# Attention, an FFT block and a gated MLP on one core: rows in six chunks of 384 instead of eight of 320 and 256, with another order of the last products and of the first loads

## The chip, the cores and the metric

The kernel runs on one NeuronCore of a Trainium2 chip. Its engines are TensorE (PE; its weight loads are shown as PEld), VectorE (DVE), ScalarE (ACT), GpSimd (POOL) and SyncE (SP), which here only issues DMAs. The metric is the device time of one execution in microseconds. Before the change the median of three runs is 808.04 us (806.26 to 809.92).

## The reference, cut to what matters

Inputs: q, k, v of (4, 8, 576, 64), weights of three parts, all float32; 4 batches of 576 rows are 2304 rows of 512 columns.

```python
scores = q @ k.T / 8;  keep 0 <= i - j < 64;  attn = softmax(scores)
x = (attn @ v) as (4, 576, 512)
u = x + real(fft(fft(x, axis=1), axis=2))
un = (u - mean(u)) / sqrt(var(u) + 1e-6)
x = u + relu(un @ w_ch1) @ w_ch2                    # 512 -> 2048 -> 512
h = gelu_tanh(x @ w_in);  g, v = h[..., :512], h[..., 512:]
v_s = w_sg @ layernorm(v) * g_ln + b_sg             # over the 576 rows of a batch
out = x + (g * v_s) @ w_out
```

## The kernel before, in words

Every product that needs full precision is made of three (`mm3`, lines 118 to 120): operands are kept as a rounded part and a remainder (`xh`, `xl` for the rows, `hi`, `lo` in the weight sets), and high x high, high x low and low x high are added up in PSUM. Rows lie transposed in SBUF: `uT` is one tile of 128 partitions x 4 x 2304 rows and holds the running sum all the way.

The rows are cut into chunks (`CHUNKS`): per batch one of 320 and one of 256, eight in all. A chunk is the moving operand of one product, so its size is the number of columns that a product streams. Each chunk has its own pair of tiles `xh[n]`, `xl[n]`.

- *Attention* (from line 248) takes blocks of 64 queries, 36 in all, in a pipeline of scores, transposes, products with v, normalization and a transpose back into `uT`. `load_q`, `load_k` and `load_v` issue all their loads from SP's queue; the mask is loaded between two pieces of the first k. Beside attention two lanes run: `weights()` decodes the first three weight sets and `work()` runs the Fourier step `dft(0)`, the layer norm `ln(0)`, `dft(1)` and `ln(1)`.
- *Layer norm* (`ln(n)`) takes a chunk in pieces of up to 128 rows: transposes of `uT` (L509), a copy, the statistics on DVE, one power on POOL, the scaling on ACT, transposes back (L528), two copies on ACT into `xh` (L531, L532) and a subtraction on POOL into `xl` (L533).
- *MLP* (`mlp`) goes by phases (`PHASES`): hidden blocks 0 to 3, then 4 and 5, over the first half of the chunks, the same over the second half, then 6 to 9, 10 to 12 and 13 to 15 over all. For each chunk and hidden block f there are 12 products into `h`, relu on ACT (L581), the remainder on DVE (L582), and, two steps later, 12 products into `acc`; at the end of a phase four adds on DVE bring `acc` into `uT` (L562). Ahead of each chunk `before(g, n)` sees to it that the chunk's layer norm has been written into the program. The lane `rest()` holds what is still missing at the start: the decode of set 3, `ln(2)` and `ln(3)` woven with `dft(2)`, `dft(3)`, and then the norms of the second half.
- *gMLP*: `gate_u` over all chunks, then per batch `v_tiles` (products of 512 columns), `spatial` (the product over a batch's 576 rows, in halves of 320 and 256, whose result goes back into `xh`, `xl`) and `project`, two chunks per batch, whose residual comes from memory (`x2`) through `ctemp` and whose result is stored from SP's queue.

The order on each engine is made by a planner when the program is built: instructions stand in the order in which the Python code emits them, moved forward by priorities (`high_priority`, `SOON`, `URGENT`), and each engine then runs its list strictly in order. `drive` only decides in which order lanes emit.

Of the kernel before, what the change touches and what calls it, by code (L numbers as in the profile page):

```python
# [20 lines left out]
NF = FF // 128  # L21
TOK = B * S
CA, CB = 320, 256
CHUNKS = [(S * b + o, n) for b in range(B) for o, n in ((0, CA), (CA, CB))]
NCH = len(CHUNKS)
P0 = 4
HEAD, TAIL = range(NCH // 2), range(NCH // 2, NCH)
PHASES = [(range(P0), HEAD), (range(P0, 6), HEAD), (range(P0), TAIL), (range(P0, 6), TAIL),
          (range(6, 10), range(NCH)), (range(10, 13), range(NCH)), (range(13, 16), range(NCH))]
URGENT = 5000  # L30
# [71 lines left out]
class Kernel:  # L102
# [101 lines left out]
    def load_k(self, b, g):  # L204
        t = self.ap_.tile([128, 4, 256], F32, tag="k", bufs=3, name="k")
        o = 192 * g
        for c in (slice(0, 128), slice(128, 256)) if b == g == 0 else (slice(0, 256),):
            self.nc.sync.dma_start(t[:, :, c], self.aps["k"][b, :, :, o + c.start:o + c.stop])
            if b == g == c.start == 0:
                self.nc.sync.dma_start(self.mask, self.aps["mask"])  # L210
        self.kt[b, g] = t

    def load_q(self, b, j, w):

        t, o = self.qring[(b * 5 + j // 2) % QB], j % 2
        for h in range(2):
            dst = t[64 * h:64 * h + 64, o:o + w, :, h].rearrange("d n a q -> d (n a) q")
            self.nc.sync.dma_start(dst, self.aps["q"][b, h, :, j:j + w].rearrange("d n a q -> d (n a) q"))
        for i in range(w):
            self.qt[b, j + i] = t[:, o + i]  # L220

# [274 lines left out]
    def ln(self, n):  # L496
        nc, p = self.nc, self.lp
        V, A = nc.vector, nc.scalar
        start, size = CHUNKS[n]
# [24 lines left out]
        for i, (o, r) in enumerate(parts):  # L524
            ps = self.gtile()
            pv = ps[:].rearrange("p (k t) -> p k t", k=4)[:, :, 0:r]
            for k in range(4):
                nc.tensor.transpose(pv[:, k], us[i][:r, 128 * k:128 * k + 128], self.ident[:r, :r])  # L528
            hi = self.xh[n][:, :, o:o + r]
# [3 lines left out]
            nc.gpsimd.tensor_tensor(out=self.xl[n][:, :, o:o + r], in0=cp, in1=hi, op=ALU.subtract)  # L533
            yield 1000


# [5 lines left out]
    def mlp(self, before):  # L542
# [26 lines left out]
        for g, (fs, ns) in enumerate(PHASES):  # L569
            for n in ns:  # L570
                before(g, n)
                xh, xl, size = self.xh[n], self.xl[n], CHUNKS[n][1]
                for f in fs:
# [4 lines left out]
                    rh = self.bp.tile([128, CA], F32R, tag="rh", bufs=3, name="rh")[:, 0:size]  # L578
                    rl = self.bp.tile([128, CA], F32R, tag="rl", bufs=3, name="rl")[:, 0:size]
# [31 lines left out]
    def ctemp(self):  # L611
        self.ndec += 1
        if self.ndec % 3 == 0:
            return self.cp.tile([128, CA], F32, tag="res", name="res")
        s = self.pers.tile([128, 256, 2], I32, tag="dec_s", bufs=2, name="dec_s")
        return s[:].rearrange("p a b -> p (a b)").bitcast(F32)[:, 0:CA]

    def ctile(self):
        self.nct += 1
# [36 lines left out]
    def v_tiles(self, b):  # L656
# [3 lines left out]
        V, A = nc.vector, nc.scalar  # L660
        o = b % 2
        if o == 0:
            for d, x in ((self.xt_h, self.xh), (self.xt_l, self.xl)):
                for e in range(2):
                    nc.gpsimd.tensor_scalar(out=d[:, :, 64 * e:64 * e + 64], in0=x[2 * (b + e)][:, :, 256:320], scalar1=1.0, scalar2=None, op0=ALU.mult)
        for i in range(5 if o == 0 else 4):
            ps = self.ctile()
            terms = []
            for k in range(4):
                if i < 4:  # L670
                    n, t = 2 * b + i // 2, slice(128 * (i % 2), 128 * (i % 2) + 128)
                    lh, ll = self.xh[n][:, k, t], self.xl[n][:, k, t]
# [25 lines left out]
    def spatial(self, b):  # L698
# [2 lines left out]
        o = b % 2  # L701
        tail = self.vtail[o]
        for h in range(2):
            n = 2 * b + h
            start, size = CHUNKS[n]
            for c in range(4):
                s = slice(128 * c, 128 * c + 128)
                ps = self.ctile()[:, 0:size]
# [5 lines left out]
                t = self.pers.tile([128, CA], I32, tag="dec_w", bufs=2, name="dec_w")[:, 0:size].bitcast(F32)  # L714
                V.scalar_tensor_tensor(out=t, in0=ps, scalar=self.gT[:, c:c + 1], in1=self.bbc[:, CA * h:CA * h + size], op0=ALU.mult, op1=ALU.add)
                V.tensor_tensor(out=t, in0=t, in1=ug, op=ALU.mult)
                A.activation(out=self.xh[n][:, c], in_=t, func=AF.Copy)
                V.tensor_tensor(out=self.xl[n][:, c], in0=t, in1=self.xh[n][:, c], op=ALU.subtract)
                yield 6 * size

    def project(self, b):
        nc = self.nc
        for h in range(2):
            n = 2 * b + h
            start, size = CHUNKS[n]
            for c in range(4):
                s = slice(128 * c, 128 * c + 128)
                res = self.ctemp()[:, 0:size]
                nc.sync.dma_start(res, self.x2[:, c, start:start + size])
                ps = self.ctile()[:, 0:size]  # L730
                self.mm3(ps, [(self.w_out(k)[0][:, s], self.w_out(k)[1][:, s], self.xh[n][:, k], self.xl[n][:, k]) for k in range(4)])
                o = self.uT[:, c, start:start + size]
                nc.vector.tensor_tensor(out=o, in0=ps, in1=res, op=ALU.add)
                if n == NCH - 1:
                    nc.sync.dma_start(self.aps["out"][:, c, start:start + size], o)
                yield 5 * size
            if n < NCH - 1:
                nc.sync.dma_start(self.aps["out"][:, :, start:start + size], self.uT[:, :, start:start + size])
# [20 lines left out]
def emit(tc, aps):  # L759
    with ExitStack() as ctx:  # L760
# [19 lines left out]
        def work():  # L780
            for b in range(2):
                yield from when(scaled(k.dft(b)), lambda: k.xdone >= b)
                yield from scaled(k.ln(b))

        def weights():
            yield W0
# [1 line left out]
                yield from spaced(k.decode_f(f), W1)  # L788

        k.open_x(0, k.lp)  # L790
        k.open_x(1, k.lp)
        fill = [[weights()], [work()]]
        drive(k.attention(), *fill)
        for f in sum(fill, []):
# [2 lines left out]
        k.attn_es.close()  # L797
        p, es = k.pool("early", side="right")
        ctx.enter_context(es)
        for n in HEAD[2:]:  # L800
            k.open_x(n, p)
        for i in (3, 4, 5):
            k.open_set(i, p)
        k.open_mlp()
# [17 lines left out]
                    else:  # L822
                        yield w / 2

        def norm(*ns):
            for n in ns:
                yield from soon(k.ln(n))
                done.add(n)

        def rest():  # L830
            yield from soon(k.decode_f(3))
            done.update((0, 1))
            yield from weave(norm(2, 3), soon(k.dft(2)))
            yield from soon(k.dft(3))
            k.dft_es.close()
            p, es = k.pool("late", side="left")
            ctx.enter_context(es)
            for n in TAIL:
                k.open_x(n, p)
            for i in (6, 7):  # L840
                k.open_set(i, p)
            for n in TAIL:
# [70 lines left out]
def layout(q, k, v, w1, w2, w_in, g, w_sg, b_sg, w_out):  # L913
# [19 lines left out]
    o["sg"] = ca(np.concatenate([st[:256], st[320:], st[256:320], st[256:320]]).reshape(5, 128, S))  # L933
    o["g"] = ca(g.reshape(4, 128).T)
    o["b"] = ca(b_sg.reshape(1, S))
    o["tab"] = tables()
# [22 lines left out]
```

## Time and profile before

| | us |
|---|---|
| median of three runs | 808.04 |
| profiled execution, its time | 806.52 |
| profiled execution, its span | 804.8 |
| TensorE busy | 780.5 |
| VectorE busy | 463.2 |
| ScalarE busy | 322.0 |
| GpSimd busy | 203.0 |

The span is the time from the first to the last instruction of the profiled execution; busy times are sums over an engine's instructions. Matmuls are pipelined: a shown duration is longer than the distance to the next one, and the distance between starts is what a product costs. "Idle before, releaser" names what ended an engine's wait.

### The profile page before, as it was taken

Reading aid. Unit: us, or ns where it says so; the run is one execution under the profiler, and the core shown is the slowest. Engines: PE = TensorE matmul, PEld = TensorE weight load, DVE = VectorE, ACT = ScalarE, POOL = GpSimd, SP = SyncE. Lnnn points to the kernel's source line nnn. Section 1 sums busy time; section 2 is a strip of 40 time slices with the busy share of each in tenths; the row PEclk is TensorE's granted clock in tenths of the full one; section 3 lists DMA queues with packets and bytes.
Section 4 is the critical chain, followed back from the end, with each engine's and each line's share of the span. In section 5 each row is a group of like instructions: output and inputs, shape, how many; then the busy total and the mean of one; then the engine's idle time right before and its main releaser. Section 6 shows DMA issues by size and latency. Waiting matters only on the chain.

```text
span 804.8 us, 15475 instructions
## 1 busy us (share of the span) xinstructions
PE 780.5 (97%) x6084; PEld 751.3 (93%) x6084; DVE 463.2 (58%) x1110; ACT 322.0 (40%) x774; POOL 203.0 (25%) x258
## 2 busy tenths in 40 slices
PE   7989699999999999999999999999999999999998
PEld 6878588989999999999999999999999998989898
DVE  4888958795286347952226823643240358565653
ACT  4877687763345434421114411333232243131310
POOL 2144536574333223310003200232250020010000
PEclk9999899999999999999999999999999999999999
DMA  8996632230021003320002400132130020303042
GB/s 252 346 272 178 180 101 68 66 104 15 2 64 43 1 15 106 118 79 1 2 1 79 131 1 1 42 115 88 44 126 11 1 60 1 118 1 118 1 118 94
DMA packets 59320, 63.70 MB, mean 79 GB/s; under 512 B 22384, under 2 KB 42736, under 8 KB 59248
## 3 DMA queue, kind: packets, MB, share of 16 engines
q1 hardware_dynamic: 58672, 59.75, 24.9%
q0 software_dynamic: 576, 2.97, 1.1%
q8 instruction: 48, 0.79, 0.4%
q14 instruction: 24, 0.20, 0.1%
HBM read 53.25 MB, written 9.44 MB: 78 GB/s over the span
## 4 chain that ended last, share of the span: by engine, by line
PE 80%; DVE 10%; DMA 4%; ACT 3%; issue 2%; SPq 1%; POOL 1%; DVEq 0%; ACTq 0%
PE acc L118 7%; PE acc L119 7%; PE acc L120 7%; PE h L118 7%; PE h L120 7%; PE h L119 7%; PE c L118 6%; PE c L119 6%; PE c L120 6%; PE g L118 3%; PE g L119 3%; PE g L120 3%; PE sc L262 3%; DMA dec_s<-in_wo 2%; PE pv L290 2%; DVE dec_w L156 2%
## 5 line engine op out<-in xcount | busy, mean ns | idle before, releaser
L118 PE MATMUL h<-xh,set 128*128 128x256 f32 (+1 forms) x512 | 151.7, 297 | 0.7 <-DVE rl L582 0.5
L118 PE MATMUL acc<-rh,set 128*128 128x256 f32 (+1 forms) x512 | 151.5, 296 | 0.8 <-DVE uT L562 0.7
L120 PE MATMUL h<-xh,set 128*128 128x256 f32 (+1 forms) x512 | 151.5, 296 | 0.0
L119 PE MATMUL h<-xl,set 128*128 128x256 f32 (+1 forms) x512 | 151.0, 295 | 0.0
L120 PE MATMUL acc<-rh,set 128*128 128x256 f32 (+1 forms) x512 | 150.8, 294 | 0.0
L119 PE MATMUL acc<-rl,set 128*128 128x256 f32 (+1 forms) x512 | 150.7, 294 | 0.0
L160 POOL TENSOR_TENSOR set<-dec_w,set 128x256 fp32r<-128x256 f32 x88 | 69.6, 797 | 230.7 <-ACT set L159 230.4
L582 DVE SCALAR_TENSOR_TENSOR rl<-h,rh 128x320 fp32r<-128x320 f32 (+1 forms) x128 | 58.0, 453 | 119.3 <-ACT rh L581 118.8
L581 ACT ACTIVATE rh<-h 128x320 fp32r<-128x320 f32 (+1 forms) x128 | 51.7, 404 | 138.9 <-PE h L120 101.5
L118 PEld LDWEIGHTS acc<-rh,set 128*128 128x128 f32 x512 | 96.5, 188 | 1.8 <-issue 1.7
L118 PEld LDWEIGHTS h<-xh,set 128*128 128x128 f32 x512 | 96.5, 189 | 1.5 <-DVE rl L582 1.4
L120 PEld LDWEIGHTS h<-xh,set 128*128 128x128 f32 x512 | 96.7, 189 | 0.0
L119 PEld LDWEIGHTS h<-xl,set 128*128 128x128 f32 x512 | 96.6, 189 | 0.0
L119 PEld LDWEIGHTS acc<-rl,set 128*128 128x128 f32 x512 | 96.4, 188 | 0.1
L120 PEld LDWEIGHTS acc<-rh,set 128*128 128x128 f32 x512 | 96.4, 188 | 0.0
L562 DVE TENSOR_TENSOR uT<-acc,uT 128x320 f32<-128x320 f32 (+1 forms) x160 | 61.8, 449 | 16.5 <-PE acc L120 16.5
L154 ACT ACTIVATE dec_g<-dec_s 128x256 f32<-128x256 f32 x88 | 38.0, 438 | 63.4 <-DVE dec_w L156 28.1
L491 POOL TENSOR_TENSOR rq<-rq,mhalf 128x1 f32<-128x1 f32 (+2 forms) x26 | 17.0, 653 | 159.7 <-DVE rq L490 156.6
L155 DVE TENSOR_SCALAR dec_w<-dec_s 128x256 int32<-128x256 int32 x88 | 36.9, 424 | 34.5 <-POOL set L160 23.0
L120 PE MATMUL c<-xh,set 128*128 128x256 f32 (+1 forms) x188 | 55.4, 295 | 0.0
L119 PE MATMUL c<-xl,set 128*128 128x256 f32 (+1 forms) x188 | 55.4, 295 | 0.0
L118 PE MATMUL c<-xh,set 128*128 128x256 f32 (+1 forms) x188 | 55.4, 295 | 0.0
(195 smaller groups left out, 1661.9 us busy)
## 6 DMA issues: line engine op xcount, KB each, us to landing
dec_s<-in_w SPq DMA_DIRECT2D x64, 256.0 KB, 2.8
v<-in_v SPq DMA_DIRECT2D x16, 520.0 KB, 4.7
k<-in_k SPq DMA_DIRECT2D x11, 512.0 KB, 5.7
dec_s<-in_wi SPq DMA_DIRECT2D x16, 256.0 KB, 2.6
q<-in_q SPq DMA_DIRECT2D x30, 128.0 KB, 5.4
x<-uT SPq DMA_DIRECT2D x4, 640.0 KB, 3.9
out<-uT SPq DMA_DIRECT2D x4, 640.0 KB, 4.0
dec_s<-in_wo SPq DMA_DIRECT2D x8, 256.0 KB, 2.8
```

The source lines that it names most:

```text
L118: mm(out, lhsT=lh, rhs=rh, start=first and i == 0, stop=False)
L119: mm(out, lhsT=lh, rhs=rl, start=False, stop=False)
L120: mm(out, lhsT=ll, rhs=rh, start=False, stop=last and i == n - 1)
L154: nc.scalar.activation(out=g, in_=s[:, :, 1].bitcast(F32), func=AF.Copy, scale=2.0 ** -112)
L155: nc.vector.tensor_scalar(out=w, in0=s[:, :, 0], scalar1=29, scalar2=None, op0=ALU.logical_shift_right)
L156: nc.vector.scalar_tensor_tensor(out=w, in0=g[:].bitcast(I32), scalar=3, in1=w, op0=ALU.logical_shift_left, op1=ALU.bitwise_or)
L160: (eng or nc.gpsimd).tensor_tensor(out=lo[:, o:o + 256], in0=f, in1=hi[:, o:o + 256], op=ALU.subtract)
L262: nc.tensor.matmul(sc[:, hp], lhsT=q[:, hp].rearrange("p a b -> p (a b)"), rhs=k[:, hp, o:o + 128], start=True, stop=True)
L491: self.nc.gpsimd.tensor_tensor(out=y, in0=v, in1=self.mhalf[:m, 0:n], op=ALU.pow)
L562: V.tensor_tensor(out=x, in0=acc[:, c, 0:size], in1=x, op=ALU.add)
L581: A.activation(out=rh, in_=o, func=AF.Relu)
L582: V.scalar_tensor_tensor(out=rl, in0=o, scalar=0.0, in1=rh, op0=ALU.max, op1=ALU.subtract)
```

## The change: what it does

Chunks become six of 384 rows, which cross the borders of the batches: chunk 1 holds the end of batch 0 and the start of batch 1, chunk 4 the end of batch 2 and the start of batch 3. Chunk 0 keeps its own tiles; chunks 1 and 2 share one pair (`open_pair`), 3 to 5 another (`open_tail`); `pieces` and `piece` find the part of a tile for a stretch of rows. `work()` no longer runs a second layer norm beside attention: `ln(1)` and `ln(2)` both stand in `rest()`, woven with `dft(2)`. `v_tiles` takes a batch's rows in plain order (the table `sg` is laid out to match), `spatial` keeps its halves and splits a result where a tile ends. `project` goes by chunk: chunk 0 after batch 0, chunks 1 and 2 after batch 1, 3 after batch 2, 4 and 5 after batch 3. The mask, and the second half of q for the first four blocks, are issued from ACT's queue.

```diff
-CHUNKS = [(S * b + o, n) for b in range(B) for o, n in ((0, CA), (CA, CB))]
+CHUNKS = [(384 * i, 384) for i in range(6)]
+X0 = 1152
+UNITS = CHUNKS
-HEAD, TAIL = range(NCH // 2), range(NCH // 2, NCH)
+HEAD, TAIL = range(3), range(3, NCH)
...
-                self.nc.sync.dma_start(self.mask, self.aps["mask"])
+                self.nc.scalar.dma_start(self.mask, self.aps["mask"])
...
-            self.nc.sync.dma_start(dst, self.aps["q"][b, h, :, j:j + w].rearrange("d n a q -> d (n a) q"))
+            eng = self.nc.scalar if h and b == 0 and j < 4 else self.nc.sync
+            eng.dma_start(dst, self.aps["q"][b, h, :, j:j + w].rearrange("d n a q -> d (n a) q"))
...
+    def open_tail(self, p):
+        h, l = (p.tile([128, 4, TOK - X0], F32R, name=f"x{x}t") for x in "hl")
+        for n in TAIL:
+            o, size = CHUNKS[n][0] - X0, CHUNKS[n][1]
+            self.xh[n], self.xl[n] = h[:, :, o:o + size], l[:, :, o:o + size]
+    def pieces(self, t0, n):
+        for a, z, tiles in ((0, 384, 0), (384, X0, 1), (X0, TOK, 2)):
+            i, j = max(t0, a), min(t0 + n, z)
+            if i < j:
...
+                yield i - t0, j - i, h[:, :, i - a:j - a], l[:, :, i - a:j - a]
...
-                A.activation(out=self.xh[n][:, c], in_=t, func=AF.Copy)
-                V.tensor_tensor(out=self.xl[n][:, c], in0=t, in1=self.xh[n][:, c], op=ALU.subtract)
+                for i, r, xh, xl in self.pieces(start, size):
+                    A.activation(out=xh[:, c], in_=t[:, i:i + r], func=AF.Copy)
+                    V.tensor_tensor(out=xl[:, c], in0=t[:, i:i + r], in1=xh[:, c], op=ALU.subtract)
...
-                yield from scaled(k.ln(b))
+                if b == 0:
+                    yield from scaled(k.ln(b))
...
-            done.update((0, 1))
-            yield from weave(norm(2, 3), soon(k.dft(2)))
+            done.add(0)
+            yield from weave(norms(1, 2), soon(k.dft(2)))
...
-            drive(k.project(b), [])
+            for n in ((0,), (1, 2), (3,), (4, 5))[b]:
+                drive(k.project(n), [])
```

## Rows read from the trace of the kernel before

**Rows 1.** The page's first part: busy time of each engine.

```profile
PE 780.5 (97%) x6084; PEld 751.3 (93%) x6084; DVE 463.2 (58%) x1110; ACT 322.0 (40%) x774; POOL 203.0 (25%) x258
```

**Rows 2.** Windows: length, busy PE, PEld, DVE, ACT, POOL, granted clock, DMA share, GB/s.

```profile
0.00:20.00 20.00, 14.87 (x107) 13.78 (x108) 9.03 (x17) 8.64 (x22) 4.88 (x21) 0.91 0.85 252
...
80.00:100.00 20.00, 12.94 (x113) 10.48 (x110) 18.21 (x39) 13.02 (x33) 10.96 (x12) 0.83 0.63 183
...
145.00:180.00 35.00, 32.91 (x243) 30.98 (x242) 31.92 (x63) 24.53 (x63) 23.27 (x25) 1.00 0.30 89
180.00:300.00 120.00, 120.00 (x918) 118.44 (x917) 64.34 (x169) 52.70 (x116) 40.52 (x48) 1.00 0.08 24
...
760.00:804.80 44.80, 41.59 (x311) 41.09 (x309) 23.06 (x60) 5.98 (x12) 1.27 (x2) 0.99 0.31 95
```

**Rows 3.** The page's groups: MLP products of line 118, both chunk sizes together.

```profile
L118 PE MATMUL h<-xh,set 128*128 128x256 f32 (+1 forms) x512 | 151.7, 297 | 0.7 <-DVE rl L582 0.5
L118 PE MATMUL acc<-rh,set 128*128 128x256 f32 (+1 forms) x512 | 151.5, 296 | 0.8 <-DVE uT L562 0.7
```

**Rows 4.** Timeline (start, duration, instruction): last project, first of 320, first and last of 256.

```profile
788.74 0.31 PE L118 MATMUL c<-xh,set 128*128 128x320 f32 x1
...
795.78 0.28 PE L118 MATMUL c<-xh,set 128*128 128x256 f32 x1
...
801.31 0.28 PE L120 MATMUL c<-xh,set 128*128 128x256 f32 x1
```

**Rows 5.** Timeline: first of 48 products of 512 in v_tiles, and the project product behind them.

```profile
670.17 0.40 PE L118 MATMUL c<-set,xh 128*128 128x512 f32 x1
...
681.30 0.31 PE L118 MATMUL c<-xh,set 128*128 128x320 f32 x1
```

**Rows 6.** Timeline of PE at the end of attention: ln(1)'s transposes, a wait.

```profile
136.17 1.10 PE L509 MATMUL g<-ident,uT 128*128 128x128 f32 x8
137.10 0.60 PE L277 MATMUL pt<-ident,s 128*128 128x128 f32 x4
...
141.13 1.12 PE L290 MATMUL pv<-v,pts 128*64 128x65 f32 x16 [1.42 <-DVE rs L494]
```

**Rows 7.** Timeline of the start: ACT's table load, SP's issues, first exponentials, a wait.

```profile
0.72 1.28 ACT L270 ACT_TABLE_LOAD   x1 [0.72 <-PEq L946]
...
0.73 1.48 SPq L218 DMA_DIRECT2D q<-in_q  x2
...
7.52 0.57 SPq L208 DMA_DIRECT2D k<-in_k  x1
...
9.07 1.28 ACT L270 ACTIVATE s<-s,mx 128x128 f32<-128x128 f32 x4 [7.06 <-DVE mx L268]
...
13.37 1.13 PE L262 MATMUL sc<-k,q 128*128 128x128 f32 x8 [1.71 <-DMA k<-in_k]
```

**Rows 8.** Timeline: ln(2)'s first transposes, its last subtraction, its chunk's first product.

```profile
144.18 1.09 PE L509 MATMUL g<-ident,uT 128*128 128x128 f32 x8
...
174.98 0.74 POOL L533 TENSOR_TENSOR xl<-u,xh 128x256 fp32r<-128x256 f32 x1
...
179.91 0.31 PE L118 MATMUL h<-xh,set 128*128 128x320 f32 x1
```

**Rows 9.** Timeline behind v_tiles(1): a project add, the last vl, the first spatial product.

```profile
686.78 0.49 DVE L733 TENSOR_TENSOR uT<-c,dec_s 128x320 f32<-128x320 f32 x1
687.34 0.69 DVE L689 TENSOR_TENSOR vl<-u,set 128x512 fp32r<-128x512 f32 x1
...
693.99 0.31 PE L118 MATMUL c<-set,set 128*128 128x320 f32 x1
```

**Rows 10.** Timeline's last add; DMA issues: count, KB each, us to landing.

```profile
801.63 0.42 DVE L733 TENSOR_TENSOR uT<-c,dec_s 128x256 f32<-128x256 f32 x1 [0.49 <-PE c L120]
...
dec_s<-x SPq DMA_DIRECT2D x10, 160.0 KB, 2.3
...
out<-uT SPq DMA_DIRECT2D x4, 128.0 KB, 2.0
```

More of the change, by code (lines that the diff above doesn't have):

```diff
@@ L23 @@
 CA, CB = 320, 256
-CHUNKS = [(S * b + o, n) for b in range(B) for o, n in ((0, CA), (CA, CB))]
+CHUNKS = [(384 * i, 384) for i in range(6)]
 NCH = len(CHUNKS)
+X0 = 1152
+UNITS = CHUNKS
+UNITS_OF = [(n,) for n in range(NCH)]
 P0 = 4
-HEAD, TAIL = range(NCH // 2), range(NCH // 2, NCH)
+HEAD, TAIL = range(3), range(3, NCH)
 PHASES = [(range(P0), HEAD), (range(P0, 6), HEAD), (range(P0), TAIL), (range(P0, 6), TAIL),
@@ L476, in open_x, with open_pair, piece @@
         self.xl[n] = p.tile([128, 4, CHUNKS[n][1]], F32R, name=f"xl{n}")
+    def open_pair(self, p):
+        h, l = (p.tile([128, 4, X0 - 384], F32R, name=f"x{x}m") for x in "hl")
+        for n in (1, 2):
+            o, size = CHUNKS[n][0] - 384, CHUNKS[n][1]
+            self.xh[n], self.xl[n] = h[:, :, o:o + size], l[:, :, o:o + size]
+        self.xmid = h, l
+    def open_tail(self, p):
+        h, l = (p.tile([128, 4, TOK - X0], F32R, name=f"x{x}t") for x in "hl")
+        for n in TAIL:
+            o, size = CHUNKS[n][0] - X0, CHUNKS[n][1]
+            self.xh[n], self.xl[n] = h[:, :, o:o + size], l[:, :, o:o + size]
+        self.xtail = h, l
+    def pieces(self, t0, n):
+        for a, z, tiles in ((0, 384, 0), (384, X0, 1), (X0, TOK, 2)):
+            i, j = max(t0, a), min(t0 + n, z)
+            if i < j:
+                h, l = ((self.xh[0], self.xl[0]), getattr(self, "xmid", None), getattr(self, "xtail", None))[tiles]
+                yield i - t0, j - i, h[:, :, i - a:j - a], l[:, :, i - a:j - a]
+    def piece(self, t0, n):
+        (_, _, h, l), = self.pieces(t0, n)
+        return h, l
     def open_set(self, i, p):
@@ L498, in ln @@
         V, A = nc.vector, nc.scalar
-        start, size = CHUNKS[n]
+        start, size = UNITS[n]
         parts = [(o, min(128, size - o)) for o in range(0, size, 128)]
@@ L528, in ln @@
                 nc.tensor.transpose(pv[:, k], us[i][:r, 128 * k:128 * k + 128], self.ident[:r, :r])
-            hi = self.xh[n][:, :, o:o + r]
+            hi, lo = self.piece(start + o, r)
             cp = us[i][:, 0:4 * r].rearrange("p (k t) -> p k t", k=4)
@@ L532, in ln @@
             A.activation(out=hi, in_=cp, func=AF.Copy)
-            nc.gpsimd.tensor_tensor(out=self.xl[n][:, :, o:o + r], in0=cp, in1=hi, op=ALU.subtract)
+            nc.gpsimd.tensor_tensor(out=lo, in0=cp, in1=hi, op=ALU.subtract)
             yield 1000
@@ L577, in mlp @@
                     self.mm3(o, [(t[:, 0, 128 * k:128 * k + 128], t[:, 1, 128 * k:128 * k + 128], xh[:, k], xl[:, k]) for k in range(4)])
-                    rh = self.bp.tile([128, CA], F32R, tag="rh", bufs=3, name="rh")[:, 0:size]
-                    rl = self.bp.tile([128, CA], F32R, tag="rl", bufs=3, name="rl")[:, 0:size]
+                    rh = self.bp.tile([128, 384], F32R, tag="rh", bufs=3, name="rh")[:, 0:size]
+                    rl = self.bp.tile([128, 384], F32R, tag="rl", bufs=3, name="rl")[:, 0:size]
                     with self.tc.high_priority(URGENT):
@@ L613, in ctemp @@
         if self.ndec % 3 == 0:
-            return self.cp.tile([128, CA], F32, tag="res", name="res")
+            return self.cp.tile([128, 512], F32, tag="res", name="res")
         s = self.pers.tile([128, 256, 2], I32, tag="dec_s", bufs=2, name="dec_s")
-        return s[:].rearrange("p a b -> p (a b)").bitcast(F32)[:, 0:CA]
+        return s[:].rearrange("p a b -> p (a b)").bitcast(F32)
     def ctile(self):
@@ L662, in v_tiles @@
         if o == 0:
-            for d, x in ((self.xt_h, self.xh), (self.xt_l, self.xl)):
-                for e in range(2):
-                    nc.gpsimd.tensor_scalar(out=d[:, :, 64 * e:64 * e + 64], in0=x[2 * (b + e)][:, :, 256:320], scalar1=1.0, scalar2=None, op0=ALU.mult)
+            for e in range(2):
+                for d, x in zip((self.xt_h, self.xt_l), self.piece(S * (b + e) + 512, 64)):
+                    nc.gpsimd.tensor_scalar(out=d[:, :, 64 * e:64 * e + 64], in0=x, scalar1=1.0, scalar2=None, op0=ALU.mult)
         for i in range(5 if o == 0 else 4):
@@ L670, in v_tiles @@
                 if i < 4:
-                    n, t = 2 * b + i // 2, slice(128 * (i % 2), 128 * (i % 2) + 128)
-                    lh, ll = self.xh[n][:, k, t], self.xl[n][:, k, t]
+                    lh, ll = (x[:, k] for x in self.piece(S * b + 128 * i, 128))
                 else:
@@ L703, in spatial @@
         for h in range(2):
-            n = 2 * b + h
-            start, size = CHUNKS[n]
+            start, size = S * b + CA * h, (CA, CB)[h]
             for c in range(4):
@@ L716, in spatial, with project @@
                 V.tensor_tensor(out=t, in0=t, in1=ug, op=ALU.mult)
-                A.activation(out=self.xh[n][:, c], in_=t, func=AF.Copy)
-                V.tensor_tensor(out=self.xl[n][:, c], in0=t, in1=self.xh[n][:, c], op=ALU.subtract)
+                for i, r, xh, xl in self.pieces(start, size):
+                    A.activation(out=xh[:, c], in_=t[:, i:i + r], func=AF.Copy)
+                    V.tensor_tensor(out=xl[:, c], in0=t[:, i:i + r], in1=xh[:, c], op=ALU.subtract)
                 yield 6 * size
-    def project(self, b):
+    def project(self, n):
         nc = self.nc
[L723 to L738, printed above, removed]
+        start, size = CHUNKS[n]
+        for c in range(4):
+            s = slice(128 * c, 128 * c + 128)
+            res = self.ctemp()[:, 0:size]
+            nc.sync.dma_start(res, self.x2[:, c, start:start + size])
+            ps = self.ctile()[:, 0:size]
+            self.mm3(ps, [(self.w_out(k)[0][:, s], self.w_out(k)[1][:, s], self.xh[n][:, k], self.xl[n][:, k]) for k in range(4)])
+            o = self.uT[:, c, start:start + size]
+            nc.vector.tensor_tensor(out=o, in0=ps, in1=res, op=ALU.add)
+            if n == NCH - 1:
+                nc.sync.dma_start(self.aps["out"][:, c, start:start + size], o)
+            yield 5 * size
+        if n < NCH - 1:
+            nc.sync.dma_start(self.aps["out"][:, :, start:start + size], self.uT[:, :, start:start + size])
 def drive(main, *lanes):
@@ L790, in emit @@
         k.open_x(0, k.lp)
-        k.open_x(1, k.lp)
         fill = [[weights()], [work()]]
@@ L799, in emit @@
         ctx.enter_context(es)
-        for n in HEAD[2:]:
-            k.open_x(n, p)
+        k.open_pair(p)
         for i in (3, 4, 5):
@@ L823, in weave, with norms, norm @@
                         yield w / 2
-        def norm(*ns):
+        def norms(*ns):
             for n in ns:
-                yield from soon(k.ln(n))
-                done.add(n)
+                yield from norm(n)
+        def norm(n):
+            for u in UNITS_OF[n]:
+                yield from soon(k.ln(u))
+            done.add(n)
         def rest():
             yield from soon(k.decode_f(3))
-            done.update((0, 1))
-            yield from weave(norm(2, 3), soon(k.dft(2)))
+            done.add(0)
+            yield from weave(norms(1, 2), soon(k.dft(2)))
             yield from soon(k.dft(3))
@@ L837, in rest @@
             ctx.enter_context(es)
-            for n in TAIL:
-                k.open_x(n, p)
+            k.open_tail(p)
             for i in (6, 7):
@@ L932, in layout @@
     st = w_sg.T
-    o["sg"] = ca(np.concatenate([st[:256], st[320:], st[256:320], st[256:320]]).reshape(5, 128, S))
+    o["sg"] = ca(np.concatenate([st, st[512:]]).reshape(5, 128, S))
     o["g"] = ca(g.reshape(4, 128).T)
```

## The prediction

> **What bounds the kernel now.** I read the page's first part, then the windows by stage, and only then the timeline. The first part shows TensorE busy 97% of the span and no other engine above 58% [rows 1]. The windows show where most of the other 24 us lie: TensorE has gaps in the attention stage (5.1 us in the first 20, 7.1 us at 80 to 100, where VectorE is busy 18.2 of 20 us), 2.1 us at 145 to 180, none from 180 to 300, and 3.2 us in the last stretch, nearly all of it the drain of the last output [rows 2]. The reader is to see that from 145 us on the time is the count of products times their spacing, at a granted clock of 1.00 (2.4 GHz): only fewer or closer products help there, and every new wait costs its full length. In the 35 us where the MLP starts VectorE is busy 31.9 us, so that is where something can come late.
>
> **1. Six chunks instead of eight.** Line 118 issues every third product of the MLP: 512 h and 512 acc over eight chunks [rows 3], so 128 per chunk; gate_u and project add 4 x 4 each by their loops; 160 times three lines make 480 products per chunk. The columns stay 2304 in all, so what can be saved is the part of the spacing that does not go with columns. From the timeline: 48 products of 320 start between 788.74 and 795.78, 146.7 ns each; those of 256 behind them take 5.53 us over 47 steps, 117.7 ns [rows 4]; 48 of 512 take 11.13 us, 231.9 ns [rows 5]. No row has 384 columns.
> - Lower bound of the spacing: 320's own surplus over its columns at 2.4 GHz (146.7 - 133.3) kept, 160 + 13.4 = 173.4 ns.
> - Between 320 and 512: 146.7 + 64 x 85.2/192 = 175.1 ns.
> - On from 256 through 320: 146.7 + 29.0 = 175.7 ns.
>
> A weight tile costs 4 x (146.7 + 117.7) = 1057.6 ns now; six of 384 cost 1040, 1051 or 1054 ns. Times 480: -8.4, -3.4 or -1.6 us. 320 is the nearest row, but its surplus grows to 18.6 ns at 512, so I take 174.5 ns: 1047 ns, **-5.1 us**. Wider relu and add instructions lie in longer steps of 4.2 us (24 x 0.1745), with more room for both; nothing is counted for them.
>
> **2. Fewer and later layer norms.** Twenty pieces of rows become 18. The two that go are those of ln(1) ahead of the MLP: 8 transposes from 136.17 to the next product at 137.10 [rows 6], and 8 back, as long: **-1.9 us**. With their VectorE steps goes part of the 1.4 us for which the products of 141.13 waited behind rs (L494) [rows 6]: 0 to -1.4, I take **-0.5 us**. What is late next there is the last pv itself.
>
> **3. The start.** SP issues one DMA after another, 6.8 us of them before the k block that the products at 13.37 wait 1.7 us for [rows 7]. Moved off SP are the mask and three q halves. A q issue is 0.74 us of SP's time (two in 1.48), so everything behind the four is issued up to 3.0 us sooner. On ACT's queue they stand behind the table load (0.72 to 2.00) and end near 5.0 us; the first activation comes at 9.07, having waited for VectorE, so ACT pays nothing. Were that cover gone, 3 us of issues would lie before the first exponential. POOL's queue is not passed by anything. The transfers share one set of engines (share 0.85 of the first 20 us [rows 2]), so the k block will not land by the whole 3 us sooner: 0 to -1.7 us (its wait gone), I take **-1.0 us**.
>
> **4. The norm that is due sooner.** Before, chunks 0 and 1 were normalized when the MLP began, and ln(2) had from 144.18 (its first transposes) to 175.72 (its last subtraction on POOL), 31.5 us; its chunk's first product came at 179.91, behind two chunks [rows 8]. Now only chunk 0 is ready, and ln(1) has to take that way while chunk 0 runs. TensorE's work before chunk 1 must begin, worked out from spacings shown above: 72 products of chunk 0, 72 x 0.1745 = 12.6 us; the 24 that normally follow later, 4.2 us, if the planner draws them ahead; dft(2)'s first stage, 39 products of 256 or 258 columns at 118 ns, 4.6 us; the norm's 24 transposes at 0.116, 2.8 us; the next norm's first eight, 0.9 us; and the start of dft(2)'s second stage, 8 products of 290 columns at some 133 ns, 1.1 us. Together 26.2 us against 31.5: a hole of 5.3 us. Of those 35 us, 2.1 are idle already [rows 2] and would fall into the hole; and without chunk 1's relu steps the norm itself should be a little sooner. Bounds: 0 (norm ready in 26 us) and +11.5 us (no work drawn ahead: 12.6 + 4.6 + 2.8 = 20.0 against 31.5). I take **+2.0 us**. Chunk 2 then has a further 16.8 us and dft's rest for ln(2), whose transposes already begin under ln(1): nothing.
>
> **5. The gMLP's order.** Spatial steps and v_tiles keep their shapes. Project's products cover the end of v_tiles: its last vl ends at 688.03, 6.7 us after the first project product at 681.30, and spatial began at 693.99 [rows 5, 9]. project(0) and project(3) are now 48 products, 8.4 us, instead of 12.7: still 1.7 us more than needed; nothing, with +1 us as the upper end. The eight extra small copies and subtractions where a spatial half crosses row 384 lie beside some 1.6 us of products each. At the end both last chunks stand behind spatial(3): chunk 4 needs only its first half, and its 8.4 us cover the chain to chunk 5. The very end grows: the add takes 0.42 us for 256 columns and 0.49 for 320 [rows 9, 10], so about 0.55; a store of 128 KB lands in 2.0 us and a load of 160 KB in 2.3 [rows 10], so 192 KB in some 2.3 to 2.6: **+0.5 us**.
>
> **Sum.** -5.1 - 1.9 - 0.5 - 1.0 + 2.0 + 0.5 = -6.0 us. The profiled execution took 806.52 us (span 804.8), 1.5 under the median of three, 808.04. The same step from each: 800.5 and 802.0. I forecast **802.0 us**, with 798 to 805.5 as this case's own range. A measurement of this kernel can tell some 0.5%, 4 us: faster is below 804.0, slower above 812.1.
>
> **Rivals.**
> - *The spacing goes with the columns, and fewer chunks save next to nothing.* For it: the surplus over 2.4 GHz is 11.0, 13.4 and 18.6 ns at 256, 320 and 512 [rows 4, 5], so a straight line through the ends leaves only 3.5 ns per product, and the line through 256 and 320 less. Against: a part per product remains in each of these lines, and it is counted 960 times. Then term 1 is -1.6 to -3.4: 804.6 us at the middle (802.0 + 2.6), no measurable change. The Trainium skill, "TensorE: Matmul & The Clock Gate", section "Back-to-back issue gap", gives columns over 2.4 GHz plus a fixed 2.5 ns; by it 960 products fewer would save 2.4 us (an estimate from that page). The trace does not agree with its size: all three rows lie 11 to 19 ns above their columns.
> - *The hole at chunk 1 decides.* One mechanism: ln(1) takes the 31.5 us of ln(2) because its steps queue between decodes on the busy VectorE, and in-order TensorE draws nothing ahead; +11.5 us there, and ln(2), pushed behind it, can be late for chunk 2 by some 4 us more. For it: VectorE's 31.9 of 35 us [rows 2]. Against: the timeline mixes dft and norm products into the MLP's freely, so the planner does draw work ahead. Beyond a hole of 10 us (my 2.0 and the 8.0 that the other terms give) the kernel is slower than before; at 15.5 us the time is 802.0 + 13.5 = 815.5.
> - *No hole and the lower spacing.* -8.4 - 1.9 - 1.4 - 1.7 + 0.5 = -12.9: 795.1 us.
> - *The wide tiles tie chunks together.* Chunks 1 and 2 share a tile, as do 3 to 5. If a wait were for the tile and not for its columns, each chunk's copy would stop the next chunk's products: 2 us or more at six chunks, +12, 814 us. Against: uT is one tile for all rows, written by adds for one chunk and read by another's norm, and the acc products waited only 0.7 us for it in the whole run [rows 3].
>
> **How the numbers follow.** Forecast 0.52; spacing rival 0.22; hole 0.12; both good 0.11; tied tiles 0.03. Faster by over 0.5%: 0.44 of the 0.52 (its range passes 804 at the upper end), 0.07 of the spacing rival and the 0.11, 0.62. Slower: 0.08 of the hole's and the 0.03, 0.11. Within 0.5%: 0.27. The range, 796 to 809, leaves out the end of the good case and holes beyond 9 us.
>
> **What would show it.** Products of 384 columns 174 to 175 ns apart; the MLP's start near 141.6 instead of 145.0; a gap before chunk 1's first product of at most a few us, with dft products and chunk 0's acc products drawn ahead of it; no gap at spatial(1) and spatial(3); 0.5 us more behind the last product. I am wrong if the spacing is above 175.5 ns, or if TensorE idles over 8 us between 142 and 200.

## The result, and the profile after

| | before | after |
|---|---|---|
| median of seven runs each, us | 807.95 (804.74 to 809.92) | 800.11 (798.43 to 803.52) |
| ratio to before, 95% interval | | 0.9916 [0.9893, 0.9938] |
| profiled execution, its time, us | 806.52 | 802.30 |
| its span, us | 804.8 | 800.5 |

The kernel is 7.8 us faster; 802.0 was forecast. The profiled execution after lies 2.2 us above its own median, the one before 1.4 below; so the two traces differ by only 4.2 us, and stages have to be compared with that in mind.

The page's first part after, against [rows 1]:

```profile
PE 774.2 (97%) x5108; PEld 744.0 (93%) x5108; DVE 455.3 (57%) x1020; ACT 314.7 (39%) x728; POOL 198.8 (25%) x248
```

976 instructions fewer on TensorE: 960 products (two chunks of 480) and 16 transposes (two pieces of rows, 8 each). The page's groups of the MLP's first product line, after [rows 3]; the two h forms of chunks 0 to 2 are left out:

```profile
L121 PE MATMUL acc<-rh,set 128*128 128x384 f32 x384 | 129.7, 338 | 0.6 <-DVE uT L594 0.3
...
L121 PE MATMUL h<-xht,set 128*128 128x384 f32 x192 | 64.8, 338 | 0.1
```

384 acc products instead of 512, and still almost no wait ahead of them. Windows after, columns and stretches as in [rows 2]:

```profile
0.00:20.00 20.00, 16.45 (x126) 15.07 (x127) 11.06 (x22) 10.17 (x28) 5.01 (x21) 1.00 0.94 257
145.00:180.00 35.00, 32.03 (x213) 30.57 (x214) 29.27 (x54) 21.89 (x53) 22.46 (x25) 0.95 0.19 62
180.00:300.00 120.00, 119.59 (x743) 117.20 (x742) 65.33 (x157) 54.33 (x113) 40.22 (x44) 1.00 0.11 36
```

TensorE does 1.6 us more in the first 20 us. From 145 to 300 it is idle 3.4 us instead of 2.1, and in 145 to 180 its granted clock averages 0.95, where it was 1.00.

The timeline at four borders after: the last 16 products with v, TAIL's first product, the last acc, the last project product (HEAD and TAIL are the two halves of the chunks):

```profile
146.94 1.12 PE L294 MATMUL pv<-v,pts 128*64 128x65 f32 x16 [0.40 <-PE g L123]
...
251.31 0.60 PE L121 MATMUL h<-xht,set 128*128 128x384 f32 x2
...
594.49 0.34 PE L123 MATMUL acc<-rh,set 128*128 128x384 f32 x1
...
796.48 0.34 PE L123 MATMUL c<-xht,set 128*128 128x384 f32 x1
```

The same borders of the kernel before:

```profile
249.67 0.39 PE L118 MATMUL h<-xh,set 128*128 128x320 f32 x1
...
598.38 0.28 PE L120 MATMUL acc<-rh,set 128*128 128x256 f32 x1
```

From TAIL's first product to the last acc the time falls from 348.71 to 343.18 us, from there to the last product ([rows 4]: 801.31) from 202.93 to 201.99. TAIL itself begins 1.6 us later in this execution. The same program profiled a second time, in the run e9 below (an added constant shifts its lines by one):

```profile
143.94 0.36 PE L295 MATMUL pv<-v,pts 128*64 128x65 f32 x3 [0.40 <-PE g L124]
...
248.36 0.60 PE L122 MATMUL h<-xht,set 128*128 128x384 f32 x2
...
591.84 0.34 PE L124 MATMUL acc<-rh,set 128*128 128x384 f32 x1
```

Here TAIL begins 1.3 us earlier than before. From the last products with v to TAIL's first product 104.37 and 104.42 us pass in these two (104.37 to 104.45 in the six executions whose order on the engines is the same: after, e1, e5, e6, e9, e10), while the last products with v start anywhere from 143.94 to 146.94. So what differs between executions of one program lies almost wholly in attention; from there on a program's stages repeat to some 0.5 us. Attention is judged by medians below, the rest by stages.

### The profile page after: what moved, and what is told of

Read it like the earlier page. It is cut to its first block, busy times and chain, and to the rows that moved or that the text cites. A ratio compares the mean times of both kernels' runs of the same rounds, so it can differ in the third digit from the quotient of the medians.

```text
span 800.5 us, 13289 instructions
## 1 busy us (share of the span) xinstructions
PE 774.2 (97%) x5108; PEld 744.0 (93%) x5108; DVE 455.3 (57%) x1020; ACT 314.7 (39%) x728; POOL 198.8 (25%) x248
## 4 chain that ended last, share of the span: by engine, by line
PE 75%; DVE 12%; DMA 6%; issue 3%; ACT 2%; SPq 1%; POOL 1%; ACTq 0%; DVEq 0%; POOLq 0%
PE acc L121 7%; PE acc L122 7%; PE acc L123 7%; PE h L121 6%; PE h L123 6%; PE h L122 6%; PE c L121 6%; PE c L123 6%; PE c L122 6%; PE g L121 3%; PE g L123 3%; PE g L122 3%; DVE dec_w L159 2%; DMA v<-in_v 2%; DMA dec_s<-in_wo 2%
## 5 line engine op out<-in xcount | busy, mean ns | idle before, releaser
L121 PE MATMUL acc<-rh,set 128*128 128x384 f32 x384 | 129.7, 338 | 0.6 <-DVE uT L594 0.3
L123 PE MATMUL acc<-rh,set 128*128 128x384 f32 x384 | 129.4, 337 | 0.0
L122 PE MATMUL acc<-rl,set 128*128 128x384 f32 x384 | 129.2, 337 | 0.0
L614 DVE SCALAR_TENSOR_TENSOR rl<-h,rh 128x384 fp32r<-128x384 f32 x96 | 53.2, 554 | 127.2 <-ACT rh L613 127.0
L613 ACT ACTIVATE rh<-h 128x384 fp32r<-128x384 f32 x96 | 46.5, 485 | 143.7 <-PE h L123 113.0
L121 PEld LDWEIGHTS acc<-rh,set 128*128 128x128 f32 x384 | 72.3, 188 | 2.0 <-issue 1.0
L123 PEld LDWEIGHTS acc<-rh,set 128*128 128x128 f32 x384 | 72.3, 188 | 0.1
L594 DVE TENSOR_TENSOR uT<-acc,uT 128x384 f32<-128x384 f32 x120 | 58.4, 549 | 19.1 <-PE acc L123 19.1
L121 PE MATMUL h<-xht,set 128*128 128x384 f32 x192 | 64.8, 338 | 0.1
L123 PE MATMUL h<-xht,set 128*128 128x384 f32 x192 | 64.6, 337 | 0.0
L122 PE MATMUL h<-xlt,set 128*128 128x384 f32 x192 | 64.5, 336 | 0.0
L160 DVE SCALAR_TENSOR_TENSOR dec_w<-dec_s,dec_w 128x256 int32<-128x256 int32 x88 | 48.8, 561 | 1.1
L159 DVE SCALAR_TENSOR_TENSOR dec_w<-dec_g,dec_w 128x256 int32<-128x256 int32 x88 | 47.0, 535 | 2.2 <-ACT dec_g L157 0.8
```

The source lines that it names most:

```text
L121: mm(out, lhsT=lh, rhs=rh, start=first and i == 0, stop=False)
L122: mm(out, lhsT=lh, rhs=rl, start=False, stop=False)
L123: mm(out, lhsT=ll, rhs=rh, start=False, stop=last and i == n - 1)
L159: nc.vector.scalar_tensor_tensor(out=w, in0=g[:].bitcast(I32), scalar=3, in1=w, op0=ALU.logical_shift_left, op1=ALU.bitwise_or)
L160: nc.vector.scalar_tensor_tensor(out=w, in0=s[:, :, 1], scalar=-2147483648, in1=w, op0=ALU.bitwise_and, op1=ALU.bitwise_or)
L594: V.tensor_tensor(out=x, in0=acc[:, c, 0:size], in1=x, op=ALU.add)
```

## The experiments

Each kernel ran four to six times. Kernels in one group shared a chip and the runs of before (nine or eleven); where a constant was added, line numbers are one higher.

**First group: one part at a time** (median of before in it: 807.26 us).

*e1: the change with its first loads back on SP's queue.*

```diff
-                self.nc.scalar.dma_start(self.mask, self.aps["mask"])
+                self.nc.sync.dma_start(self.mask, self.aps["mask"])
...
-            eng = self.nc.scalar if h and b == 0 and j < 4 else self.nc.sync
+            eng = self.nc.sync
```

> The changed kernel with the mask and all of q issued from SP again; chunks and order stay. Theory (the gain is the spacing of products, the early loads are given back as DMA waits by 40 us): the same as the changed kernel within its scatter, 799 to 802 us, 0.990 to 0.994 of before, and the products of 384 stay 174 ns apart. Rival (the earlier issue carries through): 1 to 2 us slower than the changed kernel, 801 to 803 us, with the MLP starting as much later.

Measured: 801.54 us, 0.9925 [0.9913, 0.9938]. This lies in both ranges and decides nothing; no run of the full change stood beside it on this chip.

*e2: the kernel before with only that part of the change* (the same lines the other way).

> The kernel before, with only the mask and the second half of q for the first four blocks moved to ACT's queue. Theory: the first 28 us run up to 2 us ahead, then a wait for q or v takes it back; the time is that of before within 1 us (807 to 809). Rival (the start carries through): 1 to 2 us faster, 806 to 807, and an MLP start 1 to 2 us sooner.

Measured: 804.59 us, 0.9967 [0.9954, 0.9979]. The queue alone gains 2.7 us there, more than the whole range that I gave it (0 to -1.7). That it would be given back by 40 us was wrong: the MLP's first product starts at 144.17 us, where it was 145.03. So the profiles of single executions show 0.9 of the 2.7 us there; where the rest lies is open.

*e3: the kernel before with only the second norm taken out of attention.*

```diff
-                yield from scaled(k.ln(b))
+                if b == 0:
+                    yield from scaled(k.ln(b))
...
-            done.update((0, 1))
-            yield from weave(norm(2, 3), soon(k.dft(2)))
+            done.add(0)
+            yield from weave(norm(1, 2, 3), soon(k.dft(2)))
```

> The kernel before, with ln(1) taken out of the attention stage and put ahead of ln(2) beside the MLP, eight chunks as they were. Theory (a later norm costs): 1 to 4 us slower than before, 809 to 812, with dft and norm products drawn ahead of the MLP's first product and TensorE idle 1 to 4 us more between 120 and 200. Rival (the move itself is a gain because VectorE is freed at the end of attention): 1 to 3 us faster, 805 to 807.

Measured: 813.93 us, 1.0082 [1.0068, 1.0096]: 6.7 us slower, more than either side expected. The windows of e3 where the MLP starts:

```profile
140.00:180.00 40.00, 34.55 (x277) 32.93 (x277) 32.59 (x72) 23.81 (x59) 24.55 (x27) 0.96 0.17 55
180.00:200.00 20.00, 16.52 (x127) 15.44 (x126) 15.27 (x32) 8.82 (x22) 9.00 (x11) 1.00 0.24 80
```

TensorE is idle 8.9 us in these 60; before it was 3.2 (36.78 busy up to 180, all 20 behind that by [rows 2]):

```profile
140.00:180.00 40.00, 36.78 (x280) 34.49 (x281) 34.62 (x74) 28.11 (x69) 23.81 (x28) 1.00 0.26 78
```

These 5.7 us are most of the 6.7. They are mostly not the hole of the prediction's fourth step, which was to lie ahead of chunk 1: its first product, at 163.91, waits for nothing. Of the 8.9 us, 6.3 lie behind it, the longest ahead of a relu remainder and ahead of chunk 2, whose norm ln(2) is now pushed back (its last subtraction ends at 193.57 us, before at 175.72):

```profile
176.04 0.58 PE L118 MATMUL h<-xh,set 128*128 128x256 f32 x1 [2.39 <-DVE rl L582]
...
189.33 0.46 PE L528 MATMUL g<-ident,u 64*128 64x64 f32 x4 [1.62 <-ACT bs L457]
...
193.62 0.42 PE L119 MATMUL h<-xl,set 128*128 128x320 f32 x1 [1.39 <-POOL mv L504]
```

*e4: the change with eight chunks of 288.*

```diff
-CHUNKS = [(384 * i, 384) for i in range(6)]
+CHUNKS = [(288 * i, 288) for i in range(8)]
+FIRST = 576
...
-HEAD, TAIL = range(3), range(3, NCH)
+HEAD, TAIL = range(4), range(4, NCH)
...
-            yield from weave(norms(1, 2), soon(k.dft(2)))
+            yield from weave(norms(1, 2, 3), soon(k.dft(2)))
```

> The changed kernel with eight chunks of 288 instead of six of 384: as many columns, as many products as before, everything else as changed (24 norm pieces instead of 18). Theory (what is saved is a part of the spacing that every product pays): the gain is gone; 288 columns some 133 ns apart, 8 x 133 = 1064 ns per weight tile against 1045 for six of 384, 480 x 19 = 9 us, and 3 us for six more norm pieces: 810 to 814 us. Rival (the gain is in the order of norms, loads and last products): 800 to 804 us.

Measured: 818.49 us, 1.0144 [1.0122, 1.0167], 4.5 us above the upper range. Its products of 288 stand 132.5 ns apart on average over the MLP, so eight take 1060 ns per weight tile against 1058.8 before (four each at 146.7 and 118.0) and 1044.6 after (six at 174.1). Eight chunks thus cost 480 x 15.4 = 7.4 us of products against six. Its page shows what else there is:

```profile
PE 786.8 (96%) x6116; PEld 755.4 (93%) x6116; DVE 461.3 (57%) x1118; ACT 331.6 (41%) x790; POOL 205.7 (25%) x266
```

6116 - 5108 = 1008 is 960 products and 48 transposes: six more pieces of rows, at most 48 x 0.116 = 5.6 us (eight pieces are of 32 rows only). Together some 13 of some 18 us (17.0 above e1 on the same chip, which lacks the queue's 1.2); the rest shows in the stretch where the MLP starts, 7.2 us idle in 140 to 200 and a granted clock of 0.91 in the first 40 of these:

```profile
140.00:180.00 40.00, 36.32 (x286) 34.20 (x285) 30.83 (x63) 23.38 (x58) 22.81 (x28) 0.91 0.17 57
180.00:200.00 20.00, 16.47 (x121) 14.59 (x120) 17.08 (x48) 11.54 (x25) 9.81 (x12) 1.00 0.25 80
```

So with eight chunks the rest of the change is 11.2 us slower than the kernel before: the gain, apart from the queue's, is the number of chunks and not the new layout.

**Second group: the hole at the MLP's start** (before: 807.88 us).

*e5: the change itself, as the group's measure.*

> The changed kernel itself once more, to be compared on one chip with the three others of this group. 799 to 802 us, 0.990 to 0.994 of before.

Measured: 799.61 us, 0.9908 [0.9889, 0.9926]. Its windows, and its two longest waits of TensorE in 140 to 300 us:

```profile
140.00:180.00 40.00, 37.01 (x275) 34.83 (x273) 32.89 (x64) 25.32 (x60) 24.16 (x28) 1.00 0.22 72
180.00:200.00 20.00, 18.43 (x113) 16.97 (x112) 15.63 (x39) 9.97 (x22) 7.36 (x9) 1.00 0.21 68
200.00:300.00 100.00, 100.00 (x622) 98.97 (x622) 49.56 (x118) 44.22 (x92) 32.17 (x34) 1.00 0.08 27
```

```profile
PE h L122 <- DVE rl L615: 1.8, 1, 1.8
PE g L122 <- ACT u L544: 1.2, 1, 1.2
```

TensorE is idle 4.6 us in the first 60 of these, all of it by 200 us.

*e6: relu and its remainder with a higher priority.*

```diff
-URGENT = 5000
+URGENT = 7000
```

> The changed kernel with the priority of relu, remainder and the adds raised from 5000 to 7000, above that of the norms and of dft (6000). Theory (the gap of 1.8 us at 158 and the slow clock behind it come from a remainder that stood behind folds and decodes on VectorE): that gap goes, 1 to 3 us faster than the changed kernel, 797 to 800. Rival (what is taken from the norm is paid at chunk 1, whose operand then comes later): no change or up to 3 us slower.

Measured: 799.62 us, 0.9902 [0.9883, 0.9920]. The planner made the same order of instructions on every engine as without the edit: this is the change once more and tells nothing of relu. That its time lies in the theory's range means nothing.

*e7: both norms written out ahead of dft(2).*

```diff
-            yield from weave(norms(1, 2), soon(k.dft(2)))
+            yield from norms(1, 2)
+            yield from soon(k.dft(2))
```

> The changed kernel with ln(1) and ln(2) ahead of dft(2) in the lane rest() instead of woven with it. Theory (the first products of the MLP stand behind dft(2)'s, drawn ahead of them): the MLP's first product moves from 152 towards 145, but TensorE then has less to fill a wait with at chunk 1; 0 to 3 us faster, 798 to 801. Rival (dft(2) is filling that would be missed): 1 to 5 us slower, 802 to 806, with a gap ahead of chunk 1's first product.

Measured: 802.56 us, 0.9941 [0.9923, 0.9958], 3 us slower than e5. That is in the rival's range, but without the rival's gap: chunk 1's first product, at 161.89, waits for nothing. *e8* has both edits:

> Both edits together: relu first, and the two norms ahead of dft(2). If they act on different waits, their differences from the changed kernel add up; if it is one hole that only moves, the better of the two alone is not beaten. I expect 797 to 801 us.

Measured: 801.62 us, 0.9929 [0.9909, 0.9949]; a little above its range, and the better of the two alone, e6, is not beaten. Here the priority does move a few instructions (on DVE an add and a remainder ahead of two norm steps); the 0.9 us under e7 are not clear of the scatter, as the intervals overlap. In e7 the MLP starts sooner, at 147.14 us against 151.24 in e5, but the second half's norms then come late for TAIL, which starts at 254.54 instead of 250.64. The waits of TensorE in e7 from 140 to 300 us (engine, line, what it waited for, us, times, longest):

```profile
PE pv L294 <- DVE rq L525: 1.5, 1, 1.5
PE g L560 <- ACT u L554: 1.1, 1, 1.1
PE h L121 <- DVE rl L614: 1.0, 1, 1.0
PE h L122 <- POOL xlt L565: 0.8, 1, 0.8
PE acc L121 <- DVE uT L594: 0.6, 1, 0.6
```

The wait for rl has shrunk, and rq, u (L554, a norm's), xlt and uT stand in its place. These two executions differ by only 1.0 us at the last acc (594.68 and 593.70); where the rest of the 3 us lies is not shown.

**Third group: the loads, and the hole again** (before: 806.79 us).

*e9: the change itself.*

> The changed kernel itself, for one chip with the next three. Measured 800.1 and 799.6 us so far: expected 799 to 801, 0.990 to 0.992 of the kernel before, TAIL's first product 0 to 2 us later than before's in its profile.

Measured: 800.33 us, 0.9922 [0.9905, 0.9939]. TAIL's first product came 1.3 us sooner than before's, not later as expected.

*e10: with the loads on SP's queue, as e1.*

> The changed kernel with the mask and the four q halves back on SP's queue, on one chip with the changed kernel. Theory: the earlier first loads are worth 1.0 to 1.7 us at the end of the changed kernel, as the prediction's third term said and as 2.7 us in the kernel before make likely: 800.7 to 801.5 us. Rival: what the first blocks gain is lost to the waits for q and v at 28 and 34 us, and the two kernels are within 0.5 us.

Measured: 801.53 us, 0.9934 [0.9922, 0.9946], 1.2 us above e9, as the theory had it. The two intervals overlap, so within the changed kernel this alone doesn't prove the gain; e1 points the same way, and in e2 the interval excludes no gain.

*e11: only ln(1) ahead, ln(2) woven with dft(2).*

```diff
-            yield from weave(norms(1, 2), soon(k.dft(2)))
+            yield from norms(1)
+            yield from weave(norms(2), soon(k.dft(2)))
```

> The changed kernel with ln(1) written out ahead, and only ln(2) woven with dft(2). Theory: what stands late at the MLP's start is ln(1) itself behind dft(2)'s steps, so that its chunk is ready sooner and dft(2) keeps most of its place: 797.5 to 799 us, idle PE between 100 and 200 us under 5 us. Rival: DVE's total work up to 200 us sets the end of the stage, whatever the order of norms and dft; then the time moves by less than 1 us, or up to 2.5 us slower as when both norms were written first.

Measured: 800.78 us, 0.9927 [0.9908, 0.9945], within half a microsecond of e9: the rival's answer, though idle time between 100 and 200 us did come out under 5 us (4.6). It moved; of the 3.35 and 1.87 us idle here, the second lies where the change has none:

```profile
140.00:180.00 40.00, 36.65 (x245) 35.05 (x245) 33.42 (x72) 28.13 (x65) 24.10 (x27) 1.00 0.25 80
180.00:200.00 20.00, 20.00 (x128) 19.56 (x127) 12.12 (x23) 6.84 (x16) 9.76 (x11) 1.00 0.08 27
200.00:300.00 100.00, 98.13 (x606) 96.12 (x605) 51.31 (x122) 43.75 (x91) 30.51 (x33) 1.00 0.09 27
```

*e12: the decode of sets 4 and 5 without its two reassembly steps on DVE* (those hidden blocks then get weights that aren't the true ones).

```diff
-            nc.vector.scalar_tensor_tensor(out=w, in0=g[:].bitcast(I32), ...)
-            nc.vector.scalar_tensor_tensor(out=w, in0=s[:, :, 1], ...)
+            if not light:
+                nc.vector.scalar_tensor_tensor(out=w, in0=g[:].bitcast(I32), ...)
+                nc.vector.scalar_tensor_tensor(out=w, in0=s[:, :, 1], ...)
...
-            yield from self.decode(self.aps[nm][f], t[:, 2 * i], t[:, 2 * i + 1])
+            yield from self.decode(self.aps[nm][f], t[:, 2 * i], t[:, 2 * i + 1], light=f in (4, 5))
```

> The changed kernel in which the decode of weight sets 4 and 5 leaves out its two DVE steps of reassembly (16 DVE instructions fewer, some 10 us of DVE between 140 and 200 us; the weights of these hidden blocks are then not the true ones). Theory: the hole at the MLP's start is DVE's: decodes stand ahead of chunk 0's relu remainders, so with fewer of them the hole of some 3.5 us shrinks by 1 to 3 us: 797 to 799. Rival: the hole comes from the order of the norms and dft(2), not from the decodes: 799.5 to 800.5.

Measured: 801.37 us, 0.9931 [0.9917, 0.9945]: no gain, and above both ranges. DVE's timeline in e12 ahead of chunk 0's relu remainder:

```profile
154.86 1.19 DVE L160 SCALAR_TENSOR_TENSOR dec_w<-dec_g,dec_w 128x256 int32<-128x256 int32 x2
155.97 1.86 DVE L161 SCALAR_TENSOR_TENSOR dec_w<-dec_s,dec_w 128x256 int32<-128x256 int32 x2
157.76 0.55 DVE L615 SCALAR_TENSOR_TENSOR rl<-h,rh 128x384 fp32r<-128x384 f32 x1
```

The two steps still stand there: the decode in that place isn't one of the two that were lightened. So the experiment missed the suspected steps. What it does show is that less DVE work elsewhere in the stretch (busy 15.4 us at 160 to 180, 18.1 to 19.1 in after, e5 and e9) gives no time back.

## Why the prediction was right, and where not

**1. Spacing, forecast -5.1.** Right in kind and 1.7 us small. Over the MLP after, products of 384 columns stand 174.1 ns apart, in gate_u 173.8 and in project 174.7; I took 174.5. From the timeline after, the first of 60 products up to 796.48 starts 10.31 us earlier, 59 steps of 174.7 ns:

```profile
786.17 0.33 PE L121 MATMUL c<-xht,set 128*128 128x384 f32 x1
```

Per weight tile 1044.6 ns against 1058.8, times 480, is -6.8 us at the MLP's rate. The stages agree with it but are not spacing alone: of the 5.5 us behind TAIL's start 312 weight tiles make 4.4, and the rest is the balance of 12 norm transposes fewer behind that border (36 instead of 48), 0.6 us less idle time and work that has crossed the border; of the gMLP's 1.4 us (96 weight tiles) 0.95 show, since less of gate_u now stands ahead of the last acc. The rival that spacing goes with the columns (175.1 to 175.7 ns) falls. So does the size in the Trainium skill, "TensorE: Matmul & The Clock Gate", section "Back-to-back issue gap": the fixed 2.5 ns that it gives for an isolated product would make an estimated 2.4 us of it, and the trace shows nearly three times that.

**2. Norms, -1.9 and -0.5.** The 16 transposes are gone, as counted, but one piece of the two belongs to the second half, not both to ln(1). The wait for rs of [rows 6] is gone from its place, but its 0.5 us were not gained. After, three waits of TensorE end there, 0.39 us for a copy on ACT (at 134.72), 0.40 ahead of the last products with v, and this one:

```profile
136.18 0.29 PE L121 MATMUL g<-tab,ah 128*2 128x290 f32 x1 [0.80 <-ACT bs L461]
```

Together they are 1.6 us, and 1.6 in e9 too; before it was 1.5 (1.42 and 0.12).

**3. The start, -1.0.** Right in sign; 1.2 us in e10 (where the intervals overlap), 2.7 in e2. The timeline after, against [rows 7]:

```profile
0.73 0.76 SPq L222 DMA_DIRECT2D q<-in_q  x1
0.73 0.72 ACTq L222 DMA_DIRECT2D q<-in_q  x1
...
1.49 0.61 ACTq L213 DMA_DIRECT2D mask<-in_mask  x1
...
3.44 1.28 ACT L274 ACT_TABLE_LOAD   x1 [3.44 <-issue]
...
6.32 0.57 SPq L211 DMA_DIRECT2D k<-in_k  x1
...
12.60 1.13 PE L266 MATMUL sc<-k,q 128*128 128x128 f32 x8 [0.52 <-DMA k<-in_k]
```

The issues stand ahead of ACT's table load, not behind it as I had it; it costs nothing, since the load ends at 4.72 and the first exponential, which waits for DVE, starts at 9.97. The k issue comes 1.2 us sooner, and the wait of 1.71 at 13.37 has become 0.52 at 12.60. Behind that, in this execution, the products wait 1.6 us for a q block and 1.5 for a v block, so part of it goes again; in e9 the same waits are 0.8 and 1.5, and that for k is 1.1.

**4. The hole, +2.0.** The size was near, the mechanism was not. I had ln(1) start with the MLP, at 141.6 us, run while chunk 0 does, and be late for chunk 1. Its transposes begin at 138.78, ahead of the last products with v; its last subtraction ends at 162.94; and chunk 1's first product, 8.8 us later, waits for nothing:

```profile
161.61 1.33 POOL L565 TENSOR_TENSOR xlm<-u,xhm 128x512 fp32r<-128x512 f32 x1 [0.56 <-ACT xhm L564]
...
171.78 0.34 PE L121 MATMUL h<-xhm,set 128*128 128x384 f32 x1
```

So that some idle time of the forecast size appeared is luck. The MLP starts at 151.99 (e9: 148.98), since some 4 us of dft(2)'s and ln(1)'s products are drawn ahead of the last products with v, and more between them and the first h. The gap is in chunk 0. TensorE after:

```profile
157.69 0.45 PE L121 MATMUL acc<-rh,set 128*128 128x384 f32 x1 [0.24 <-ACT rh L613]
159.97 0.44 PE L121 MATMUL h<-xh,set 128*128 128x384 f32 x1 [1.83 <-DVE rl L614]
...
161.09 0.52 PE L123 MATMUL h<-xh,set 128*128 128x384 f32 x1
161.41 0.52 PE L121 MATMUL h<-xh,set 128*128 128x384 f32 x1
```

and beside it ACT and DVE:

```profile
157.17 0.47 ACT L613 ACTIVATE rh<-h 128x384 fp32r<-128x384 f32 x1
```

```profile
156.46 1.19 DVE L159 SCALAR_TENSOR_TENSOR dec_w<-dec_g,dec_w 128x256 int32<-128x256 int32 x2
157.58 1.86 DVE L160 SCALAR_TENSOR_TENSOR dec_w<-dec_s,dec_w 128x256 int32<-128x256 int32 x2
159.37 0.55 DVE L614 SCALAR_TENSOR_TENSOR rl<-h,rh 128x384 fp32r<-128x384 f32 x1
```

rh is ready at 157.64, but DVE has a pair of decode steps in hand since 157.58, so rl starts at 159.37 and the next h only at 159.97; then, behind that wait, ten products stand 0.32 us apart, 384 columns at the lower clock of 1.2 GHz. In e5 the clock stays at 1.00 (140 to 200 us), and the idle time of 140 to 200 us is 4.6 us against 3.2 before: +1.3 us. That DVE's order makes this wait is read from rows; no run took the steps away from that place, so it isn't shown by experiment. In e7 and e11 another order of norms and dft only moved the idle time. Why a late norm costs 6.7 us in e3 and about 1.3 here is not shown by a run either, but rows point at ln(2): in e3, e4 and after, 192 products of the first two chunks stand ahead of chunk 2's first. They take 25.4 us with 320 and 256 columns or with 288, and 33.4 us with 384, so six chunks give ln(2) 8.0 us more. From 140 to 200 us e3 idles 8.9 us and e4 7.2, against 4.6 in e5 and 3.4 in e9. How much of the difference this makes stays open.

**5. The gMLP, +0.5.** Right: 4.02 us from the last product to the end of the span, 3.49 before. No wait stands at the spatial steps.

**The sum.** With what was measured or counted: -6.8, -1.9 (16 transposes at 0.116), 0 for the wait, -1.2, +1.3, +0.5 give -8.1, against -7.8, -8.3 and -6.5 between the medians of the result, e5 and e9. The 1.6 us to the last are within what attention varies from one execution to the next. So the forecast of -6.0 was 1.8 us small, for the most part by the spacing. Of the rivals, the one in which the hole decides comes nearest in e3: with eight chunks the idle time is real, though ahead of chunk 2; with six it is not there. No wait on a wide tile appears: from 200 to 300 us TensorE is busy all 100 us in e5.

## What to carry to other kernels

Where TensorE is the bound, price a change of tile width by the measured spacing at several widths: the part that doesn't go with columns (two products fewer saved 14.2 ns for each weight tile here) is paid at every product and so adds up to microseconds, and fewer row pieces save their transposes besides. A norm that is moved later is not free even when the engine has other work: test the move alone (here +6.7 us) before trusting that the rest of the change covers it. And compare two profiles from a border behind the stage that varies, and whole kernels by medians: here the profiles showed 4.2 us of a gain of 7.8.

## What the runs showed of the hardware

- A wait and a lower clock can stand for each other. After the 1.83 us wait the granted clock fell in the profiles of after, e9 and e10 (0.96 over 140 to 180 us) and not in those of e1, e5 and e6 (1.00), all of the same order. e5 then waited 1.2 us for ACT's u instead, and all six took 104.4 us from the last products with v to TAIL.
- Four small loads moved from SP's queue to ACT's gained 2.7 us in the kernel before, although the k block of [rows 7] was issued only 1.8 us sooner (at 5.75 us instead of 7.52).
- What varies between executions of one program here is above all attention: the last products with v started up to 3.0 us apart, while TAIL's first product to the last acc took 343.0 to 343.5 us, and the 202.0 us from the last acc to the last product repeated to 0.01.
